# Softmax normalisation of an attention block split between VectorE and GpSimd, and spectra held back behind the last block of powers

## The chip, the cores and the metric

The kernel runs on one core of one Trainium2 chip. A core has engines that run side by side, each with an instruction queue of its own that it works through in order: TensorE (PE in the profile; PEld is its weight load), VectorE (DVE), ScalarE (ACT), GpSimd (POOL) and SyncE (SP), which here only issues DMAs. They wait for each other through semaphores. SBUF is the working memory. PSUM is the small memory that TensorE writes its results to. The metric is the device time of one execution in microseconds (us).

## The reference, cut to what matters

Two independent results stand side by side in the output. Both are over a sequence of 2048 positions and 448 channels, in float32.

```python
# A: a diagonal state-space model as a long convolution
dt = exp(log_dt); A = -exp(log_A_real) + 1j * A_imag
C = (C_real + 1j * C_imag) * dt[:, None]
P = exp((A * dt[:, None])[:, :, None] * pos)          # 448 x 256 x 2048 powers
K = 2.0 * einsum("dn,dnl->dl", C, P).real             # the kernel of the convolution
y = irfft(rfft(u, 2 * L) * rfft(K, 2 * L), 2 * L)[:L] + u * D_skip
# B: attention with 16 heads of 28
q, k, v = split(x @ wqkv)
p = softmax(q @ k.T * 28 ** -0.5)                     # per head, 2048 x 2048
out_B = (p @ v) @ wo
out = concatenate([y, out_B], axis=-1)
```

## The kernel before, in words

**Before the loop** the projections q, k and v and small tables ("seeds" of the powers, kept in DRAM as `sd`) are made. Nothing of that is touched.

**The loop** has 256 slots (variable `s`). Attention is cut into 16 units of 16 slots: unit `u` is a group of four heads (`u // 4`, four groups) and a quarter of the queries (`u % 4`, 512 queries). A slot takes 128 keys: four score matmuls (`pss`), four exponentials on ScalarE (`p`), and the sixteen matmuls with the values of the slot before (`po`). In the same slots the maxima of the scores of a later unit are found: four matmuls into `pm`, reduced on DVE (`mx`, `rl`). `pm` is a ring of three PSUM buffers in the loop, from `w_tile()`, which all other small matmuls share.

**Powers.** Between the attention work the kernel of the convolution is built in 56 blocks of 8 channels, one every 3.5 slots. For a block, ScalarE copies seeds into `e` and `g`. GpSimd then doubles `e` three times, with three instructions each time (`e_power`, line 689): `e<-e,sdb`, `eu<-e,sdb`, `e<-e,eu`, with 256, 512 and 1024 elements in each partition. So a block is nine GpSimd instructions. DVE does the like for `g`. Four slots after the block began, TensorE multiplies them (`pm<-e,g`, line 739), in two slots. The last block, 55, begins in slot 193.

**The end of a unit.** `fin` (line 789) copies the unit's sums `po` into `o`, whose layout has 32 rows for each head: 28 outputs and the denominator. Two functions are put in the list `free`, with the number of the call of `slot()` from which they are due; there are two such calls in a slot, three late in the loop. `sums` turns `o` in 32x32 squares on DVE (`rb<-o`), so that the denominators stand in columns, and takes the reciprocals `r`. `scale`, two calls later, turns the reciprocals back with DVE (`pm<-r`, into a ring buffer of PSUM), multiplies (`on<-o,pm`, DVE), and either stores `on` in DRAM (units 0 to 11) or puts the output projection in the list `p_due` (units 12 to 15, the last head group, `pm<-ua,og` and `pm<-ua,on`).

**Spectra and final transforms.** From slot 192 on, 16 jobs of kind `s` multiply the spectra of `u` and of the kernel (`spectrum`, line 828), and 8 jobs of kind `f` transform back (`finish`, line 871). A spectrum job makes `pm<-yk,mw` on TensorE twice, `pr<-pm,ub` on DVE, four products `p<-pr,pr` on GpSimd and `pm<-p,mw` on TensorE, whose result is stored. A final transform has a skip product `ut<-ut,dsk` on GpSimd and matmuls `pm<-zi,wb`. `f_slot` (line 980) takes the next task of such a job if the call of `slot()` had nothing more urgent.

**What sets the order.** In the loop every engine's instructions stay in the order in which the code issues them (`KEPT["a"]`, line 89). An engine may run ahead of the others, but never past an instruction of its own that waits. The lists `powers["e"]` and `powers["g"]` hold what is left of a block's powers; `k_due` holds the blocks that haven't begun.

Of the kernel before, what the change touches and what calls it, by code (L numbers as in the profile page):

```python
# [8 lines left out]
F32 = mybir.dt.float32  # L9
# [3 lines left out]
ALU = mybir.AluOpType  # L13
# [13 lines left out]
NK = L // 128  # L27
# [13 lines left out]
UG = (2, 2, 4)  # L41
# [51 lines left out]
def body(ctx, tc, a, out):  # L93
    nc = Engines(tc)
# [4 lines left out]
    def pool(stack, name, bufs=1, space=None, side=None):  # L99
        kw = {} if space is None else {"space": space}  # L100
        if side:
            kw["side"] = side
        return stack.enter_context(tc.tile_pool(name=name, bufs=bufs, reuse_waits="tile", **kw))
# [23 lines left out]
    def w_tile():  # L127

        n_ring[0] += 1
        return ps_w[0].tile([128, CQ], F32, name=f"pm{n_ring[0] % ps_w[1]}")  # L130
# [7 lines left out]
    def mm32(o, w, x_, start, stop, at=0):  # L138

        for i in range(w.shape[-1] // 32):  # L140
            c = slice(32 * i, 32 * i + 32)
            nc.tensor.matmul(o[c], w[:, c], x_, start=start, stop=stop, tile_position=(0, at + 32 * i))
# [467 lines left out]
    kq_p = pool(kq_st, "kq_p")  # L610
# [178 lines left out]
    def fin(u, s_):  # L789
        g, c = divmod(u, NQ)  # L790
        o = kq_p.tile([128, CQ], F32, name="o")
        nc.scalar.activation(o, o_u[u], AF.Copy)
        on = kq_p.tile([128, CQ], F32, name="on", bufs=2)
        og = og_u.pop(u, None)
        t_ = {}

        def sums():
            t = kq_p.tile([128, NK, 32], F32, name="rb")
            nc.vector.transpose(t.rearrange("p b e -> p (b e)"), o)
            t_["r"] = kq_p.tile([128, NK], F32, name="r", bufs=2)  # L800
            nc.vector.reciprocal(t_["r"], t[:, :, DH])

        def scale():
            pw = w_tile()
            nc.vector.transpose(pw.rearrange("p (b e) -> p b e", e=32), t_["r"][:, :, None].to_broadcast([128, NK, 32]))
            nc.vector.tensor_tensor(on, o, pw, ALU.mult)
            if g < G - 1:
                nc.sync.dma_start(on_d[c][g], on)
            else:
                p_due.extend((s_ + PD + PS * t, lambda t=t: project(t)) for t in range(4))  # L810

        def project(t):
            pw = w_tile()
            ts = slice(t * 128, (t + 1) * 128)
            for g2 in range(G):
                mm32(pw[:, :D], og[:, g2, ts] if g2 < G - 1 else on[:, ts], wo_t[g2 // 2][:, g2 % 2, :],
                     start=g2 == 0, stop=g2 == G - 1)
            y = kq_p.tile([128, D], F32, name="y", bufs=2)
            nc.scalar.activation(y, pw[:, :D], AF.Copy)
            q0 = c * CQ + t * 128  # L820
            nc.sync.dma_start(out[q0:q0 + 128, D:], y)

        free.append((n_slot[0] + UG[1], sums))
        free.append((n_slot[0] + UG[2], scale))

    fk = {}

# [83 lines left out]
    def job(j, p, uh_p, ps, b0=(2, 1, 1, 2, 2), b1=(2, 2)):  # L911
        kind, f, i = j
        return spectrum(f, i, p, uh_p, ps, b0) if kind == "s" else finish(f, i, p, ps, b1)
# [10 lines left out]
    urgent, free = collections.deque(), collections.deque()  # L924
    powers = {"g": collections.deque(), "e": collections.deque()}
# [20 lines left out]
    k_due = collections.deque(range(NB))  # L946
# [7 lines left out]
    n_slot, f_next = [0], {"s": 0, "f": 0}  # L954
# [6 lines left out]
    def f_load(s_, kind):  # L961

        if not f_jobs[kind] or f_loaded[kind]:
            return
        _, f, i = f_jobs[kind][0]
        if kind == "f" and s_done[0] < (f + 1) * N1 // 4:
            return
        if (kind, f, i) == ("f", 0, 0):
            if f_ready["s", 1] == NS:
                return  # L970
            f_p["f", 0] = f_p["f", 1] = pool(f1_st, "ff_p")
        if (kind, f) not in f_p or f_ready.get((kind, f), 0) > s_ + 2:
            return
        load, tasks, ahead = job(f_jobs[kind].popleft(), f_p[kind, f], kq_p, w_tile)
        load()
        if ahead:
            f_ahead.append((s_ + FL[kind] - 1, ahead))
        f_loaded[kind].append((max(f_ready.get((kind, f), 0), s_ + FL[kind]), tasks))

    def f_slot(s_, kind):  # L980
        f_load(s_, kind)
        while f_ahead and f_ahead[0][0] <= s_:
            f_ahead.popleft()[1]()
        if not f_tasks[kind]:
            if not f_loaded[kind] or f_loaded[kind][0][0] > s_:
                return False
            f_tasks[kind].extend(f_loaded[kind].popleft()[1])
            f_load(s_, kind)
        gap, t = f_tasks[kind][0]
        if n_slot[0] < f_next[kind] + gap:  # L990
            return False
        f_tasks[kind].popleft()
        t()
        s_done[0] += kind == "s" and not f_tasks[kind]
        f_next[kind] = n_slot[0]
        f_load(s_, kind)
        return True
# [10 lines left out]
    def slot(s_):  # L1008
        n_slot[0] += 1
        while free and free[0][0] <= n_slot[0]:  # L1010
            free.popleft()[1]()
        if urgent and urgent[0][0] <= n_slot[0]:
            urgent.popleft()[2]()
        elif s_ >= NS and f_slot(s_, "s"):
            pass
        elif p_due and p_due[0][0] <= s_:
            p_due.popleft()[1]()
        elif m_due and m_due[0][0] <= s_:
            m_due.popleft()[1]()
        elif u_due and u_due[0][0] <= s_:  # L1020
            u_part(*u_due.popleft()[1:])
        else:
            f_slot(s_, "s") or f_slot(s_, "f")
# [35 lines left out]
    for s in range(NS):  # L1059
# [26 lines left out]
        for op in ORDER:  # L1086
            if op[0] == "s":
                ps.append(s_mm(u, kt, int(op[1])))
            elif op[0] == "f":
                slot(s)  # L1090
            elif op[0] == "v":
                vec()
            elif op == "k":
                k_next()
                k_begin(s)
                k_seed(s)
                for _ in range(3):
                    if powers["e"]:
                        powers["e"].popleft()()
            elif op == "pv":  # L1100
                if prev:
                    pv_step(*prev)
                    if prev[1] == NK - 1:
                        fin(prev[0], s)
            elif sm < NS:
                max_mm(sm // NK, sm % NK, int(op[1]))
# [9 lines left out]
        prev = (u, kt, ps)  # L1116
    pv_step(*prev)
    fin(prev[0], NS)
    s = NS
    while urgent or free or p_due or m_due or u_due or any(q[k] for q in (f_jobs, f_tasks, f_loaded) for k in "sf"):  # L1120
# [61 lines left out]
```

## Time and profile before

| what | value |
|---|---|
| median of 3 runs | 1279.68 us (1278.78 to 1281.36) |
| the profiled execution | 1280.71 us |
| its span | 1278.9 us |
| granted TensorE clock, mean | 0.982 |
| DVE multiply `on<-o,pm` | 16 x 0.687 us |
| DVE transpose `pm<-r` | 16 x 0.720 us |
| POOL powers, a block | 9 instructions, 11.9 us (block 9: 349.54 to 361.43) |

A row of an engine in order of time reads: start in us from the span's start, length in us, engine, line, operation, output<-inputs, partitions x elements, how often; in brackets the idle time of the engine before it and whose work ended that wait. All work is issued through helpers, so every row has the line 77, and the names tell what it is. A row of the list by line has the busy time of all and the mean in ns, and behind the second bar the idle time before. A row of the list of waits reads: who waited for whom, us in total, times, longest.

### The profile page before, as it was taken

The page shows a single profiled execution, that of the slowest core. Times are in us where ns is not written, and L with a number is a line of the kernel's source. Part 1 is how long each engine was busy: PE and PEld are TensorE (multiplying, and loading weights), DVE is VectorE, ACT ScalarE, POOL GpSimd, SP SyncE. Part 2 cuts the span into 40 slices and gives each one's busy share as a digit, 9 for nine tenths or more (in the row PEclk, how much of TensorE's full clock was granted, in tenths as well). Part 3 has the DMA queues.
Part 4 walks back from the last instruction along what each step waited for, and adds up shares of the span by engine and source line. Part 5 has one row for each costly group of instructions (what it writes and reads, how often), then busy time and mean ns, then how long its engine had stood idle before and what let it go on. Part 6 is the DMA issues. An engine that isn't in the chain of part 4 may idle for free.

```text
span 1278.9 us, 31211 instructions
## 1 busy us (share of the span) xinstructions
PE 1199.8 (94%) x11569; PEld 669.9 (52%) x11569; DVE 942.6 (74%) x2138; ACT 959.2 (75%) x2146; POOL 843.5 (66%) x728
## 2 busy tenths in 40 slices
PE   6778887999999999999999999999997999999998
PEld 4667664555555555555555555555553545545333
DVE  5788966878777878887789889888996665646312
ACT  5888865788888888888888888888885766756553
POOL 2666740897788888778599999889984222424321
PEclk8999899899999999999999999999998999999999
DMA  6678789437554545365533133422314443647666
GB/s 195 215 254 297 268 287 358 120 88 195 155 147 115 164 118 178 110 228 178 170 88 104 49 88 103 148 82 71 99 43 141 157 161 135 210 151 236 201 179 164
DMA packets 203377, 206.08 MB, mean 161 GB/s; under 512 B 98201, under 2 KB 162265, under 8 KB 201177
## 3 DMA queue, kind: packets, MB, share of 16 engines
q1 hardware_dynamic: 202696, 203.50, 51.6%
q8 instruction: 91, 1.49, 0.5%
q10 hardware_dynamic: 528, 0.59, 0.2%
q14 instruction: 62, 0.50, 0.1%
HBM read 121.59 MB, written 82.18 MB: 159 GB/s over the span
## 4 chain that ended last, share of the span: by engine, by line
PE 72%; DVE 13%; POOL 5%; ACT 4%; issue 3%; DMA 2%; ACTq 0%; SPq 0%; POOLq 0%; DVEq 0%
PE pm L77 40%; PE pss L77 15%; PE po L77 15%; DVE mx L77 2%; DVE tri L77 2%; ACT rl L77 1%; ACT p L77 1%; DVE rl L77 1%; POOL qhat L77 1%; DVE g L77 1%; DVE zg L77 1%; POOL p L77 1%; DMA xn<-in_B_x 1%; POOL e L77 1%; PE pt L77 1%
## 5 line engine op out<-in xcount | busy, mean ns | idle before, releaser
L77 ACT ACTIVATE p<-pss 128x512 f32<-128x512 f32 x1024 | 561.9, 610 | 127.6 <-PE pss L77 124.3
L77 PE MATMUL pss<-qhat,khat 128*128 128x512 f32 x1024 | 402.0, 399 | 2.0 <-ACT p L77 2.0
L77 DVE TENSOR_REDUCE mx<-pm 128x1 f32<-128x512 f32 x480 | 308.2, 683 | 102.1 <-PE pm L77 100.5
L77 PE MATMUL pm<-khat,qhat 128*128 128x512 f32 x749 | 327.0, 440 | 14.3 <-DVE mx L77 5.4
L77 POOL TENSOR_TENSOR e<-e,sdb 128x256 f32<-128x256 f32 x168 | 201.9, 1202 | 110.8 <-ACT e L77 101.6
L77 PE MATMUL po<-p,v 128*32 128x512 f32 x2048 | 269.6, 595 | 0.0
L77 PEld LDWEIGHTS pm<-khat,qhat 128*128 128x128 f32 x749 | 140.9, 188 | 231.1 <-ACT p L77 53.7
L77 POOL TENSOR_TENSOR e<-e,eu 128x256 f32<-128x256 f32 x168 | 248.2, 1477 | 13.2
L77 DVE CUSTOM_DVE_ANT_0 rl<-pm,rl 128x512 f32<-128x512 f32 x259 | 178.1, 688 | 68.1 <-ACT rl L77 65.8
L77 PEld LDWEIGHTS pss<-qhat,khat 128*128 128x128 f32 x1024 | 190.4, 188 | 45.5 <-issue 11.4
L77 POOL TENSOR_TENSOR eu<-e,sdb 128x256 f32<-128x256 f32 x168 | 202.0, 1202 | 0.0
L77 POOL TENSOR_TENSOR p<-pr,pr 64x448 f32<-64x448 f32 x64 | 73.1, 1142 | 149.1 <-PE pm L77 108.1
L77 ACT ACTIVATE rl<-pm 128x512 f32<-128x512 f32 x259 | 156.7, 606 | 15.6 <-PE pm L77 9.4
L77 DVE TENSOR_TENSOR g<-g,zg 128x128 f32<-128x128 f32 x392 | 162.0, 413 | 3.5
L77 PE MATMUL pm<-kdif,qhat 128*128 128x512 f32 x249 | 100.0, 402 | 6.7 <-DVE xn L77 4.3
L77 PE MATMUL pm<-xh,khat 128*128 128x512 f32 x256 | 84.4, 422 | 11.9 <-DVE hl L77 5.1
L77 DVE TENSOR_TENSOR zg<-g,zg 128x128 f32<-128x128 f32 x224 | 87.9, 393 | 5.0
L77 PE MATMUL pm<-e,g 128*32 128x64 f32 x3584 | 73.7, 223 | 10.7 <-POOL e L77 8.2
L77 PEld LDWEIGHTS pm<-e,g 128*32 128x32 f32 x3584 | 56.0, 110 | 49.1 <-POOL e L77 12.5
L77 DVE TENSOR_TENSOR pr<-pm,ub 128x448 f32<-128x448 f32 x64 | 36.8, 618 | 45.8 <-PE pm L77 30.3
L77 ACT ACTIVATE y<-pm 128x448 f32<-128x448 f32 x48 | 26.6, 555 | 58.4 <-PE pm L77 32.8
L77 ACT ACTIVATE ub<-pm 128x224 f32<-128x224 f32 (+1 forms) x96 | 38.6, 448 | 40.0 <-PE pm L77 38.1
(132 smaller groups left out, 1406.1 us busy)
## 6 DMA issues: line engine op xcount, KB each, us to landing
sdb<-sd SPq DMA_DIRECT2D x55, 336.0 KB
qhat<-q SPq DMA_DIRECT2D x64, 256.0 KB
khat<-k SPq DMA_DIRECT2D x64, 256.0 KB
sd<-sg SPq DMA_DIRECT2D x8, 1456.0 KB
k<-hl SPq DMA_DIRECT2D x16, 512.0 KB
mw<-in_mw SPq DMA_DIRECT2D x16, 512.0 KB
sd<-qhat SPq DMA_DIRECT2D x8, 896.0 KB
yu_d<-ub SPq DMA_DIRECT2D x64, 112.0 KB
```

What stands on the lines that cost most here:

```text
L77: i = f(*args, **kw)
```

## The change

Three things are different.

1. `scale` is cut in two. `spread` comes at the call at which `scale` came, and turns the reciprocals back with DVE as before, but into SBUF (the buffer `rb`, which `sums` has used just before) and no longer into a PSUM buffer of the ring.
2. `scale` comes one call of `slot()` later and multiplies on GpSimd (`on<-o,rb`). The store of `on`, or the output projection, follows it there.
3. `f_slot` still loads what a spectrum or a final transform needs, but takes up no task as long as a block of powers is due or has instructions left.

```diff
+        def spread():
+            t_["rb"] = kq_p.tile([128, NK, 32], F32, name="rb")
+            nc.vector.transpose(t_["rb"], t_["r"][:, :, None].to_broadcast([128, NK, 32]))
+
         def scale():
-            pw = w_tile()
-            nc.vector.transpose(pw.rearrange("p (b e) -> p b e", e=32), t_["r"][:, :, None].to_broadcast([128, NK, 32]))
-            nc.vector.tensor_tensor(on, o, pw, ALU.mult)
+            nc.gpsimd.tensor_tensor(on, o, t_["rb"].rearrange("p b e -> p (b e)"), ALU.mult)
             if g < G - 1:
                 nc.sync.dma_start(on_d[c][g], on)
             else:
...
         free.append((n_slot[0] + UG[1], sums))
-        free.append((n_slot[0] + UG[2], scale))
+        free.append((n_slot[0] + UG[2], spread))
+        free.append((n_slot[0] + UG[2] + 1, scale))
...
     def f_slot(s_, kind):
         f_load(s_, kind)
+        if k_due or powers["e"] or powers["g"]:
+            return False
         while f_ahead and f_ahead[0][0] <= s_:
             f_ahead.popleft()[1]()
```

DVE's queue at the end of unit 1, before the change (numbers behind a name tell buffers apart):

```order
L77 TENSOR_TENSOR g_4318<-g_4318,zg_4390 128x32x8
L77 ISA rl_4497,mx_4134<-pm1_4503,rl_4497 128x512
L77 ISA mx_4134 128x1
L77 TENSOR_TENSOR g_4318<-g_4318,zg_4390 128x32x16
L77 STREAM_TRANSPOSE pm2_4511<-r_4436 128x512
L77 TENSOR_TENSOR on_4374<-o_4372,pm2_4511 128x512
L77 TENSOR_TENSOR zg_4390<-g_4318,zg_4390 128x256
```

In the changed program the transpose stands at the same place, with `rb` as its output, and the row with `on_4374` is gone from DVE. It is in GpSimd's queue, between the second and the third doubling of block 9:

```order
 L77 TENSOR_TENSOR eu_4472<-e_4255,sdb_3863 128x32x16
 L77 TENSOR_TENSOR e_4255<-e_4255,eu_4472 128x32x16
+L77 TENSOR_TENSOR on_4374<-o_4372,rb_4511 128x512
 L77 TENSOR_TENSOR e_4255<-e_4255,sdb_3863 128x32x32
 L77 TENSOR_TENSOR eu_4535<-e_4255,sdb_3863 128x1024
```

Three instructions of block 9 are now behind `on`, which reads what DVE's transpose writes. In the other units up to 11 it stands likewise ahead of the first, the fourth or the seventh instruction of a block.

GpSimd's queue at the last block of powers, 55 (`e_14134`), where unit 11 ends and the first spectrum's products (`p0`, `p1`) stood:

```order
 L77 TENSOR_TENSOR eu_14263<-e_14134,sdb_13785 128x32x8
 L77 TENSOR_TENSOR e_14134<-e_14134,eu_14263 128x32x8
+L77 TENSOR_TENSOR on_14193<-o_14191,rb_14304 128x512
 L77 TENSOR_TENSOR e_14134<-e_14134,sdb_13785 128x32x16
-L77 TENSOR_TENSOR eu_14351<-e_14134,sdb_13785 128x32x16
-L77 TENSOR_TENSOR e_14134<-e_14134,eu_14351 128x32x16
-L77 TENSOR_TENSOR p0_14414<-pr00_14345,pr11_14412 64x448
-L77 TENSOR_TENSOR p0_14414<-pr01_14347,pr10_14410 64x448
-L77 TENSOR_TENSOR p1_14417<-pr00_14345,pr11_14412 64x448
-L77 TENSOR_TENSOR p1_14417<-pr01_14347,pr10_14410 64x448
+L77 TENSOR_TENSOR eu_14332<-e_14134,sdb_13785 128x32x16
+L77 TENSOR_TENSOR e_14134<-e_14134,eu_14332 128x32x16
```

The four products now stand behind the whole block, and `on` of unit 11 ahead of its second doubling.

GpSimd's queue at the end of the program, in the change (`ut` are the skip products of the last final transforms):

```order
L77 TENSOR_TENSOR ut_17429<-ut_17429,dsk_16067 128x896
L77 TENSOR_TENSOR ut_17512<-ut_17512,dsk_16067 128x896
L77 TENSOR_TENSOR ut_17609<-ut_17609,dsk_16067 128x896
L77 TENSOR_TENSOR ut_17704<-ut_17704,dsk_16067 128x896
L77 TENSOR_TENSOR on_17746<-o_17744,rb_17760 128x512
L1184 UNCONDITIONAL_BRANCH
```

Before, the last `ut` was GpSimd's last work, and `on_17746` was DVE's.

## The prediction

> **What bounds the kernel now.** I read the page first, then who waited for whom, then the rows of single engines in order of time. The span and the busy shares:
>
> ```profile
> span 1278.9 us, 31211 instructions
> PE 1199.8 (94%) x11569; PEld 669.9 (52%) x11569; DVE 942.6 (74%) x2138; ACT 959.2 (75%) x2146; POOL 843.5 (66%) x728
> PE 72%; DVE 13%; POOL 5%; ACT 4%; issue 3%; DMA 2%; ACTq 0%; SPq 0%; POOLq 0%; DVEq 0%
> ```
>
> TensorE is busy for 94% and holds 72% of the chain that ended last. So an instruction that is moved between DVE and GpSimd is worth what it changes in TensorE's waits, not its own length. The waits that the change can touch:
>
> ```profile
> POOL e L77 <- ACT e L77: 101.6, 26, 39.8
> PE pm L77 <- POOL e L77: 8.2, 3, 6.5
> PE pm L77 <- DVE on L77: 4.4, 10, 0.7
> ```
>
> GpSimd's powers (`e`) wait for ScalarE's seeds 26 times: GpSimd runs ahead of its place in the program, by data. TensorE waits for powers only three times, 6.5 us of it once, and ten times, 4.4 us, for DVE's `on`, which holds one of three PSUM buffers.
>
> **Two DVE instructions become one, and one GpSimd instruction is added, 16 times.** The rows of the pair that the change takes apart, by line:
>
> ```profile
> L77 DVE STREAM_TRANSPOSE pm<-r 128x512 f32<-128x512 f32 x16 | 11.5, 720 | 0.0
> L77 DVE TENSOR_TENSOR on<-o,pm 128x512 f32<-128x512 f32 x16 | 11.0, 687 | 0.5
> L77 DVE STREAM_TRANSPOSE rb<-o 128x512 f32<-128x512 f32 x16 | 11.3, 705 | 1.1 <-ACT o L77 1.1
> ```
>
> The transpose stays, now into SBUF; the last row is a like transpose into SBUF, 0.705 us, so I keep 0.72. The multiply leaves DVE: 16 x 0.69 = 11.0 us, worth only what TensorE waited for it. On GpSimd its price is not in the trace. The nearest row is a 128x512 of the powers in the block of rows below, and is taken up there.
>
> **What stands behind the new instruction.** GpSimd works in order. That is seen where two clears wait behind TensorE:
>
> ```profile
> 626.77 0.85 POOL L77 MEMSET ua<- 128x896 f32 x1
> 638.78 0.85 POOL L77 MEMSET ua<- 128x896 f32 x1 [11.16 <-PE pm L77]
> ```
> ```profile
> 663.41 0.65 PE L77 MATMUL pm<-e,g 128*32 128x64 f32 x32 [1.33 <-POOL e L77]
> ```
>
> Two blocks of powers stand behind the second one; the later of them came 1.33 us too late for TensorE. The new `on` is such an instruction: it waits for DVE's transpose, and in units 0 to 11 powers are queued behind it, nine instructions to a block. One block's rows (block 9; instructions 1, 4, 6, 7 and 9):
>
> ```profile
> 349.54 0.63 POOL L77 TENSOR_TENSOR e<-e,sdb 128x256 f32<-128x256 f32 x1 [3.80 <-ACT e L77]
> 351.65 1.05 POOL L77 TENSOR_TENSOR e<-e,sdb 128x512 f32<-128x512 f32 x1
> 353.81 1.31 POOL L77 TENSOR_TENSOR e<-e,eu 128x512 f32<-128x512 f32 x1
> 355.19 1.91 POOL L77 TENSOR_TENSOR e<-e,sdb 128x1024 f32<-128x1024 f32 x1
> 359.05 2.38 POOL L77 TENSOR_TENSOR e<-e,eu 128x1024 f32<-128x1024 f32 x1
> ```
>
> The price of `on` first: a dense 128x512 takes 1.31 us (third row), one with a broadcast operand 1.05 (second). Both operands of `on` are dense, so I take 1.31. The block ends at 361.43. What is left of it is 11.89 us from its first instruction, 9.78 from the fourth, 6.24 from the seventh. The order of the changed program gives the place of `on`: ahead of the seventh of block 9 (unit 1), the fourth of 14 (unit 2), the fourth of 23 (unit 4), the first of 28 (unit 5), the seventh of 32 (unit 6), the first of 37 (unit 7), the seventh of 41 (unit 8), the fourth of 46 (unit 9), the fourth of 55 (unit 11).
>
> DVE's multiply in the trace starts 0.02 us after the transpose ended, so its start tells when GpSimd's may begin. These starts, units 1, 2, 4 to 9 and 11:
>
> ```profile
> 365.78 0.69 DVE L77 TENSOR_TENSOR on<-o,pm 128x512 f32<-128x512 f32 x1
> 430.39 0.69 DVE L77 TENSOR_TENSOR on<-o,pm 128x512 f32<-128x512 f32 x1
> 557.76 0.69 DVE L77 TENSOR_TENSOR on<-o,pm 128x512 f32<-128x512 f32 x1
> 622.06 0.69 DVE L77 TENSOR_TENSOR on<-o,pm 128x512 f32<-128x512 f32 x1
> 683.55 0.69 DVE L77 TENSOR_TENSOR on<-o,pm 128x512 f32<-128x512 f32 x1
> 739.98 0.69 DVE L77 TENSOR_TENSOR on<-o,pm 128x512 f32<-128x512 f32 x1
> 797.30 0.69 DVE L77 TENSOR_TENSOR on<-o,pm 128x512 f32<-128x512 f32 x1
> 854.78 0.69 DVE L77 TENSOR_TENSOR on<-o,pm 128x512 f32<-128x512 f32 x1
> 968.70 0.69 DVE L77 TENSOR_TENSOR on<-o,pm 128x512 f32<-128x512 f32 x1
> ```
>
> In unit 1 GpSimd went on to the seventh instruction at 355.19; now it must wait until 365.8. TensorE's first use of a block's powers, for blocks 9, 14, 23, 28, 32, 38, 42, 46 and 55:
>
> ```profile
> 371.90 0.65 PE L77 MATMUL pm<-e,g 128*32 128x64 f32 x32
> 440.11 0.65 PE L77 MATMUL pm<-e,g 128*32 128x64 f32 x32
> 567.82 0.65 PE L77 MATMUL pm<-e,g 128*32 128x64 f32 x32
> 636.42 0.65 PE L77 MATMUL pm<-e,g 128*32 128x64 f32 x32
> 689.39 0.65 PE L77 MATMUL pm<-e,g 128*32 128x64 f32 x32
> 762.98 0.65 PE L77 MATMUL pm<-e,g 128*32 128x64 f32 x32
> 813.26 0.65 PE L77 MATMUL pm<-e,g 128*32 128x64 f32 x32
> 864.11 0.65 PE L77 MATMUL pm<-e,g 128*32 128x64 f32 x32
> 987.42 1.08 PE L77 MATMUL pm<-e,g 128*32 128x64 f32 x32 [6.46 <-POOL e L77]
> ```
>
> The powers are ready at the start of `on` in the list, plus 1.5 us (1.31 and about 0.2 for three handovers), plus what is left of the block. Against TensorE's use:
> - unit 1: 365.78 + 1.5 + 6.24 = 373.52, late by 1.62
> - unit 2: 430.39 + 1.5 + 9.78 = 441.67, late by 1.56
> - unit 4: 557.76 + 1.5 + 9.78 = 569.04, late by 1.22
> - unit 5: 622.06 + 1.5 + 11.89 = 635.45, early by 0.97
> - unit 6: 683.55 + 1.5 + 6.24 = 691.29, late by 1.90
> - unit 7: block 38 follows block 37 without a gap, so 739.98 + 1.5 + 2 x 11.89 = 765.26, late by 2.28
> - unit 8: block 42 follows 41, so 797.30 + 1.5 + 6.24 + 11.89 = 816.93, late by 3.67
> - unit 9: 854.78 + 1.5 + 9.78 = 866.06, late by 1.95
>
> Units 0, 3 and 10 leave more room than unit 5. The seven late ones sum to **+14.2 us**, in which the loss of their waits for DVE is already counted. In units 0, 3, 5 and 10 those waits fall away for nothing in exchange: nine of 0.42 on average stand in the loop (4.4 less the last, 0.62, over nine), three of them in units 3, 5 and 10: **-1.3 us**. The next thing late there is DVE's transpose itself, which stays. On SP's queue the stores of `on` move back one slot; nothing behind them is needed within a slot.
>
> **The spectra that start later.** Before, the first spectrum's products came between the last block's powers:
>
> ```profile
> 968.75 0.96 PE L77 MATMUL pm<-yk,mw 128*32 128x224 f32 x16 [0.37 <-DVE pm L77]
> 976.35 4.77 POOL L77 TENSOR_TENSOR p<-pr,pr 64x448 f32<-64x448 f32 x4 [12.93 <-DVE pr L77]
> 987.00:992.00 5.00, 4.58 (x58) 2.26 (x59) 0.00 (x0) 0.53 (x2) 0.37 (x1) 0.56 0.00 0
> ```
>
> GpSimd held the last three powers of block 55 for 12.93 us until DVE's products came; TensorE stood 6.46 us and then ran at a granted clock of 0.56 (the row of the stretch from 987 to 992; the clock stands behind the busy times). With the spectra behind the powers this goes, but unit 11's `on` now stands ahead of the fourth instruction: 968.70 + 1.5 + 9.78 = 979.98. That is 7.4 us sooner than 987.42. Two groups of spectrum matmuls, about 0.9 us each, are moved behind it and are still to be done: 5.6 is left. The slow stretch costs 5 x (1 - 0.56) = 2.2 us; TensorE now waits at most 3 us there, nearest to the 1.33 us wait at 663.41, after which the same matmuls took 0.65 as always, so I count 2.2 as won. The two groups will meet the three PSUM buffers where they go: 1.0 us back (0.37 and two like it). Together **-6.8 us**, between -4 and -9.
>
> The Trainium skill ("TensorE: Matmul & The Clock Gate", Part 1) says that the clock falls to half after about 3.4 us without work. The rows fit: half after 6.46 us, full after 1.33, with nothing between them in the loop. By the page the new waits stay below it and the sum is the same; if unit 8's 3.67 us came in one piece it would add some 2 us by the page, but it falls on two blocks.
>
> In the changed order the last spectrum ends in slot 246 instead of 245, and from slot 249 TensorE's row of work is the same, so the moved work costs nothing unless its store is late for the first final transform.
>
> **The end.** For the last unit DVE's `on` let TensorE go at 1262.79; GpSimd has the skip product before it:
>
> ```profile
> 1260.36 2.09 POOL L77 TENSOR_TENSOR ut<-ut,dsk 128x896 f32<-128x896 f32 x1 [4.49 <-DVE ot L77]
> 1262.79 0.96 PE L77 MATMUL pm<-ua,on 128*32 128x448 f32 x8 [0.62 <-DVE on L77]
> ```
>
> 1262.45 + 1.31 + 0.14 = 1263.9: **+1.1 us**, all on the path. For units 12 to 14 `on` is needed only behind the matmuls of the three earlier head groups and has no powers behind it; it costs nothing, and without that cover 0.6 us a unit, the difference between the two multiplies.
>
> **The sum.** 14.2 - 1.3 - 6.8 + 1.1 = +7.2 us on the span of 1278.9. The profiled execution took 1280.71, 1.03 above the median of 1279.68; I put the difference on the median: 1286.9 us.
>
> **The rivals.**
> - *DVE turns the reciprocals sooner than the trace says* (place: the transpose ahead of `on`, units 1 to 9). Each microsecond sooner takes one from each of seven waits and adds one to the gain of unit 11, about 8 us in all, so from 0.9 us on the kernel is no longer slower; at 1.5 us it would take 1279.68 + 7.2 - 12 = 1274.9. For it: DVE has less to do. Against it: its transpose has 0.0 idle before it, and what it lost stands behind the transpose, not before it. 9%.
> - *GpSimd's `on` takes longer or is let go later than 0.1 us after the transpose.* By 0.5 us: 8 x 0.5 = +4, 1290.9. For it: DVE and GpSimd then work on SBUF at once. Against it: the powers keep 1.31 beside any DVE work. 14%.
> - *The change does not put the powers behind a wait, because GpSimd passes waiting instructions.* Then 1279.68 - 1.3 - 2.5 (the other six waits) - 6.8 + 1.1 = 1270.2. The clear at 638.78 speaks against it. 2%.
> - *The late spectra lengthen the end*: the first final transform of the second half waits for the last store; one slot, 3.3 us: 1290.2. 8%.
>
> **How the numbers follow.** The forecast has 67%, and itself runs from 1282 to 1291: 1.05 instead of 1.31 takes 7 x 0.26 = 1.8, the gain at block 55 moves by 2.8 either way. The range for 8 in 10 takes in most of the two slower rivals and the first half of the first: 1280 to 1292.5. About 0.2%, 2.6 us, is what a measurement of this kernel can tell from no change. Slower by more: most of the forecast and the two slower rivals, 83%; within it 8%; faster 9%, from the first and third rival.
>
> **What would show it.** GpSimd's `on` should stand with waits of 3 to 11 us for DVE ahead of it in units 0 to 11, and TensorE's waits for `e` should rise from 8.2 to some 18 us in about ten pieces, the largest below 4. Around the last block no wait of 6 us and no clock of 0.56. TensorE's waits for DVE's `on` should be gone, and the last one should be for GpSimd's. It is wrong if TensorE's use of a block is later than here by itself, or if DVE's transposes move.

## The result, and the profile after

The changed kernel takes 1296.08 us (median of 4 runs, 1294.2 to 1296.8), the kernel before 1280.49 us beside it (4 runs, 1278.78 to 1281.36). The ratio is 1.0122, with a 95% interval of 1.0109 to 1.0135: 15.6 us slower. Predicted were 1286.9 us, in a range that ended at 1292.5. The direction was right, and the size only half of what it is.

The head of the page of the kernel after (busy shares, then shares of the chain that ended last):

```profile
span 1294.2 us, 31215 instructions
...
PE 1203.9 (93%) x11569; PEld 672.9 (52%) x11569; DVE 932.7 (72%) x2122; ACT 959.5 (74%) x2146; POOL 861.8 (67%) x744
...
PE 64%; DVE 12%; POOL 10%; ACT 4%; issue 4%; DMA 4%; SPq 1%; ACTq 0%; POOLq 0%; DVEq 0%
```

GpSimd's busy time rose from 843.5 to 861.8 us, DVE's fell from 942.6 to 932.7, and GpSimd's share of the chain rose from 5% to 10%. What GpSimd does more is little; what counts is what TensorE waits for behind it. From the list of waits of the kernel after (who waited for whom, us in total, times, longest):

```profile
POOL on L77 <- DVE rb L77: 59.0, 9, 10.7
...
PE pm L77 <- POOL e L77: 21.9, 12, 2.8
...
PE pm L77 <- POOL on L77: 4.5, 2, 3.2
```

GpSimd waited 59.0 us in front of its multiply until DVE's transpose ended, and 23.1 us more in four waits that the list puts down to other engines. TensorE's waits for powers rose from 8.2 to 21.9 us in twelve pieces, its waits for DVE's `on` (4.4 us before) are gone, and two new ones, for GpSimd's `on`, are there. GpSimd's rows in order of time, kernel after, end of unit 1 (the last three rows are what is left of block 9):

```profile
352.55 1.30 POOL L77 TENSOR_TENSOR e<-e,eu 128x512 f32<-128x512 f32 x1
364.44 1.28 POOL L77 TENSOR_TENSOR on<-o,rb 128x512 f32<-128x512 f32 x1 [10.59 <-DVE rb L77]
365.67 1.91 POOL L77 TENSOR_TENSOR e<-e,sdb 128x1024 f32<-128x1024 f32 x1
...
369.54 2.34 POOL L77 TENSOR_TENSOR e<-e,eu 128x1024 f32<-128x1024 f32 x1
```

This is as predicted: 10.59 us of waiting, 1.28 us of work (1.31 was taken), and the block ends at 371.88 instead of 361.43. TensorE's rows behind it, kernel after:

```profile
371.93 0.65 PE L77 MATMUL pm<-e,g 128*32 128x64 f32 x32 [2.14 <-POOL e L77]
372.40 1.70 PE L77 MATMUL po<-p,v 128*32 128x512 f32 x8
373.85 1.74 PE L77 MATMUL pm<-ua,w 128*32 128x448 f32 x8
...
378.29 1.04 PE L77 MATMUL po<-p,v 128*32 128x512 f32 x8
```

TensorE waited 2.14 us. And then the same eight matmuls `po<-p,v` took 1.70 us that take 1.04 us one slot later. The clock says why: stretches of 4 us in both kernels (busy us of PE, PEld, DVE, ACT and POOL with counts, granted clock, DMA share, GB/s), first before, then after:

```profile
374.00:378.00 4.00, 4.00 (x54) 2.38 (x51) 3.03 (x7) 3.51 (x8) 0.31 (x2) 1.00 0.48 146
```
```profile
374.00:378.00 4.00, 4.00 (x32) 1.89 (x28) 1.61 (x3) 1.96 (x4) 3.84 (x4) 0.74 0.28 95
...
444.00:448.00 4.00, 4.00 (x16) 2.41 (x8) 2.08 (x5) 1.94 (x6) 3.76 (x5) 0.57 0.27 102
...
696.00:700.00 4.00, 4.00 (x46) 2.38 (x39) 1.43 (x3) 1.31 (x4) 3.77 (x6) 0.61 0.19 64
...
816.00:820.00 4.00, 4.00 (x57) 2.12 (x49) 2.77 (x6) 2.77 (x7) 3.77 (x5) 1.00 0.01 2
```

Behind the waits of 2.14, 2.17 and 2.46 us (blocks 9, 14 and 32) the granted clock fell to half for a while; behind one of 2.66 us, at 814.95, it stayed full. In the row from 444 the loss is 4 x (1 - 0.57) = 1.7 us. Each fall costs about that, and the three together 5.2 us, by the same working over all stretches of 4 us of the loop. The kernel before lost nothing there.

**Where the 15.3 us of the span are.** ScalarE's copy `o<-po` marks the end of each unit in both traces. The difference of its start to the kernel before tells how late a unit is, and the change of that difference what a stretch cost. The start at unit 0 itself moves by -0.97 to +0.62 us from run to run; that is scatter. For the end of unit 11, ScalarE's row of the kernel before, then of the kernel after:

```profile
961.09 0.71 ACT L77 ACTIVATE o<-po 128x512 f32<-128x512 f32 x1
```
```profile
975.68 0.73 ACT L77 ACTIVATE o<-po 128x512 f32<-128x512 f32 x1
```

At unit 0 the kernel after was 0.97 us early and here it is 14.59 late, so the loop cost 15.56. Every run of this study is cut up in this way (us against the trace of before; the last column is what the stretches and the start at unit 0 sum to):

| kernel | units 0 to 11 | 11 to 12 (block 55) | 12 to 13 | 13 to 14 | 14 to the end | span |
|---|---|---|---|---|---|---|
| after | +15.56 | -7.00 | +0.69 | +5.29 | +1.73 | +15.3 |
| e1: spectra alone | +0.02 | -10.55 | +0.95 | +0.96 | +0.89 | -8.2 |
| e2: GpSimd alone | +15.87 | +0.86 | +3.83 | -0.28 | +7.10 | +27.4 |
| e3: multiply 8 calls later | -7.12 | -11.28 | +0.67 | +1.69 | +1.96 | -14.0 |
| e4: last four units on DVE | +15.53 | -7.00 | +0.64 | +1.24 | +1.62 | +12.4 |
| e5: multiply 1 call later | -6.79 | -11.23 | +0.70 | +5.11 | +2.21 | -10.0 |
| e6: multiply 1 call earlier | +15.61 | -6.92 | +1.74 | +1.13 | +2.42 | +14.1 |
| e7: waits filled | +11.08 | -8.36 | +0.70 | +4.31 | +4.59 | +12.3 |
| e8: 8 calls later, last four on DVE | -7.14 | -11.28 | +0.92 | +1.02 | +2.11 | -15.0 |
| e9: DVE, both operands in SBUF | +4.01 | -9.65 | +1.00 | +2.29 | +1.73 | 0.0 |
| e10: e8 again | -7.00 | -11.26 | +0.91 | +1.17 | +1.89 | -14.1 |

### The profile page after: what moved, and what is told of

It reads as the page before. It is cut to its first block, busy times and chain, and to the rows that moved or that the text cites. A ratio compares the mean times of both kernels' runs of the same rounds, so it can differ in the third digit from the quotient of the medians.

```text
span 1294.2 us, 31215 instructions
## 1 busy us (share of the span) xinstructions
PE 1203.9 (93%) x11569; PEld 672.9 (52%) x11569; DVE 932.7 (72%) x2122; ACT 959.5 (74%) x2146; POOL 861.8 (67%) x744
## 4 chain that ended last, share of the span: by engine, by line
PE 64%; DVE 12%; POOL 10%; ACT 4%; issue 4%; DMA 4%; SPq 1%; ACTq 0%; POOLq 0%; DVEq 0%
PE pm L77 37%; PE po L77 13%; PE pss L77 13%; POOL e L77 4%; DVE mx L77 2%; DVE tri L77 2%; ACT rl L77 1%; POOL eu L77 1%; ACT p L77 1%; DVE rl L77 1%; POOL qhat L77 1%; DMA ut<-in_A_u 1%; DVE g L77 1%; DMA xn<-in_B_x 1%; DVE zg L77 1%
## 5 line engine op out<-in xcount | busy, mean ns | idle before, releaser
L77 PEld LDWEIGHTS pss<-qhat,khat 128*128 128x128 f32 x1024 | 192.1, 190 | 46.2 <-issue 10.6
L77 PE MATMUL pm<-e,g 128*32 128x64 f32 x3584 | 73.7, 223 | 21.9 <-POOL e L77 21.9
L77 POOL TENSOR_TENSOR on<-o,rb 128x512 f32<-128x512 f32 x16 | 20.6, 1285 | 82.2 <-DVE rb L77 59.0
```

The lines of the kernel that those rows point to most:

```text
L77: i = f(*args, **kw)
```

## The experiments

**The two halves alone.** First only the later spectra, with the softmax as before:

```diff
     def f_slot(s_, kind):
         f_load(s_, kind)
+        if k_due or powers["e"] or powers["g"]:
+            return False
```

> Only the third part of the change: the spectra wait until no block of powers is due or has instructions left; the multiply stays on DVE as before. Theory (waiting in GpSimd's queue): TensorE's wait of 6.46 us at block 55 and the slow clock behind it go, so about 9 us faster than before, less 1 to 2 us late in the loop where the later spectra meet: about 1273 us. Rival (the later spectra are what costs time at the end, from unit 12 on): the trace of the change lost 7 us from unit 12 to the end, and all of it would appear here: about 1279 us.

Measured: 1272.3 us, 0.9933 (0.9917 to 0.995). Then only the multiply on GpSimd, without these two lines:

> Only the first two parts: reciprocals into SBUF, multiply on GpSimd a slot later; spectra as before. Theory: the loss of units 0 to 10, 15.6 us, stays whole, and the stall at block 55 stays about as it was since the products hold the queue anyway; with unit 13 and the last unit, 3 to 6 us more: 1298 to 1302 us. Rival (the two parts of the change disturb each other and neither alone costs much): below 1290 us.

Measured: 1308.09 us, 1.0211 (1.0196 to 1.0226). So the loss belongs to the multiply, and the later spectra win: 8 to 9 us alone, 12 us beside the GpSimd multiply (1308.09 - 1296.08). The second run is 6 us slower than the expected range. In its trace `on` stands behind four spectrum products at units 12 and 14, TensorE waits 2.22 and 3.38 us for it, and the granted clock falls behind both; the stretches 12 to 13 and 14 to the end lost 3.8 and 7.1 us. TensorE at block 55 in e2:

```profile
1003.25 1.08 PE L77 MATMUL pm<-e,g 128*32 128x64 f32 x32 [6.47 <-POOL e L77]
```

The stall of the kernel before (6.46 us) is still there, and the matmuls behind it take 1.08 us, as before, in the place of 0.65. So it is the spectra's place that takes the stall away. In e1 the stretch of block 55 won 10.55 us; from unit 12 on it gave 2.8 back, with these waits of e1:

```profile
PE pm L77 <- POOL p L77: 3.3, 4, 1.4
...
PE pm L77 <- DMA zi<-z: 0.7, 1, 0.7
```

TensorE waits for GpSimd's spectrum products, four times, and once for a load of the first final transforms: the rival of the late spectra, in part.

**The queue's place.** In units 0 to 11 the multiply was put eight calls further back, behind the blocks of powers, everything else as in the change:

```diff
-        free.append((n_slot[0] + UG[2] + 1, scale))
+        free.append((n_slot[0] + UG[2] + (9 if g < G - 1 else 1), scale))
```

> The change with GpSimd's multiply of units 0 to 11 queued eight calls (four slots) later; the same instructions on the same engines, only the place in GpSimd's queue differs. Theory: DVE's transpose is then done when GpSimd comes to the multiply, no wait for DVE stands ahead of it, TensorE's waits for powers fall from 21.9 us to under 3 and the clock stays full in the loop; units 0 to 10 gain 15 to 19 us on the change and block 55 another 2 to 4: 1274 to 1279 us. Rival (GpSimd's longer multiply, or SBUF shared by DVE and GpSimd, is what slows the loop): the place doesn't matter, 1290 us or more.

Measured: 1267.53 us, 0.9899 (0.9885 to 0.9914), faster than expected. Next only one call, half a slot, further back (`+ 2` in the place of the 9):

> The change with GpSimd's multiply of units 0 to 11 one call (half a slot) later than in the change. In GpSimd's queue it then stands three instructions of the powers later: ahead of the fourth of block 5, the first of 10, the seventh of 14, 23, 46 and 55, the first of 33 and 42, the fourth of 37. Theory (powers queued behind the wait, priced as in the prediction: start in DVE's list + 1.5 us + what is left of the block): block 10 ready at 379.2 for 383.9, block 14 at 438.1 for 440.1, 23 at 565.5 for 567.8, 33 at 696.9 for 703.1, 42 at 810.7 for 813.3, 46 at 862.5 for 864.1, only block 38 late, by 0.2; so all of TensorE's waits of over 1.5 us go, and the clock with them: 1266 to 1270 us, like the multiply four slots later. Rival (the wait only shrinks by the half slot, about 1.9 us in each of seven places, and the clock still falls at the longest): 1275 to 1283 us.

Measured: 1270.0 us, 0.9919 (0.9904 to 0.9934). GpSimd's rows at the end of unit 1 in e5, and then the waits of e5:

```profile
365.37 1.28 POOL L77 TENSOR_TENSOR on<-o,rb 128x512 f32<-128x512 f32 x1 [4.45 <-PE pm L77]
366.61 0.64 POOL L77 TENSOR_TENSOR e<-e,sdb 128x256 f32<-128x256 f32 x1
```
```profile
POOL on L77 <- DVE rb L77: 31.4, 8, 6.0
...
PE pm L77 <- POOL e L77: 1.3, 1, 1.3
```

The first row names TensorE, but DVE's transpose had only just ended, at 365.22. Half a slot moved `on` from the middle of block 9 to the start of the next block. GpSimd still waits 31.4 us for the transpose at its multiply, but TensorE's waits for powers fell from 21.9 to 1.3 us. The same instruction on the same engine costs 26.1 us more or less (1296.08 - 1270.0), by what is queued behind it alone. The loop is 6.8 to 7.1 us faster than before in e3 and e5, where the sum had counted on 3.8 at most (TensorE's waits for DVE's `on` in the loop).

**The waits themselves or the clock.** TensorE got seven more matmuls ahead of the first use of `e` in seven late blocks. Their result is overwritten by the next matmul into the same buffer, so nothing is left out:

```diff
+FILL = (9, 14, 23, 32, 41, 46, 55)
...
+            if i == 0 and b in FILL:
+                u = now[0]
+                for _ in range(7):
+                    nc.tensor.matmul(pw, kt_g[u // NQ][0][:, :128], q_u[u][:, 0, :], start=True, stop=True)
...
+        now[0] = u
```

> The change with seven more score matmuls (about 1.6 us of TensorE work, written to the buffer that the block's own matmuls then overwrite) ahead of the first use of the powers of blocks 9, 14, 23, 32, 41, 46 and 55. More work for TensorE and no shorter wait for the powers. Theory (the waits of 2 to 3 us let TensorE's clock fall to half for 3.4 us, 1.7 us each, three times in the loop and once at block 55 in the change's trace): the work fits into the waits, the clock stays full, and the time falls by 5 to 7 us, to about 1290 us. Rival (the slow matmuls behind the waits are not the clock that follows idleness, or the added work meets no wait): the same as the change, or up to 11 us slower.

Measured: 1291.93 us, 1.0086 (1.0068 to 1.0103). With 49 matmuls more the kernel is 4.2 us faster than the change. TensorE at block 9 in e7, and then three stretches of e7, columns as above:

```profile
372.91 0.65 PE L78 MATMUL pm<-e,g 128*32 128x64 f32 x32 [0.56 <-POOL e L78]
373.38 1.04 PE L78 MATMUL po<-p,v 128*32 128x512 f32 x8
```
```profile
374.00:378.00 4.00, 4.00 (x56) 2.15 (x52) 2.07 (x4) 2.61 (x6) 3.77 (x5) 1.00 0.55 164
...
444.00:448.00 4.00, 4.00 (x54) 2.41 (x51) 3.27 (x9) 2.97 (x7) 3.84 (x4) 1.00 0.08 30
...
696.00:700.00 4.00, 4.00 (x52) 2.43 (x51) 3.90 (x11) 3.48 (x9) 3.84 (x4) 1.00 0.23 70
```

The powers come as late as in the change (TensorE's use at 372.91 instead of 371.93, with unit 0 ending 0.95 us later), but the clock is 1.00 in all three and `po<-p,v` takes 1.04 us. The loop cost 11.08 instead of 15.56 us, 4.5 less, near the 5.2 that the clock had taken. A part of that win was lost at the last unit, where TensorE waited 3.28 us for `on` behind the skip product and the clock fell.

**The last head group.** Two ways to take GpSimd's skip product from the path of `on` in units 12 to 15. In the first, DVE multiplies there, and GpSimd elsewhere:

```diff
-            nc.gpsimd.tensor_tensor(on, o, t_["rb"].rearrange("p b e -> p (b e)"), ALU.mult)
+            (nc.gpsimd if g < G - 1 else nc.vector).tensor_tensor(on, o, t_["rb"].rearrange("p b e -> p (b e)"), ALU.mult)
```

> The change with the multiply of units 12 to 15 back on DVE, still one call after the transpose into SBUF. Theory (at unit 13 the multiply waits on GpSimd behind a skip product that waits for a DMA): the wait of 3.19 us and the slow clock behind it go, and about 0.6 us at the very end: 5 to 6 us faster than the change, about 1290.5 us. Rival (the loss around unit 13 comes from the shifted spectra, not from the multiply): the same as the change within 1 us.

Measured: 1292.96 us, 1.0094 (1.0074 to 1.0115), 3.1 us less than the change and not 5 to 6; the intervals of the two overlap. The stretch from unit 13 to 14 did fall, by 4.05 us, but the profiled run was 1.3 us later at unit 0, which the edit does not touch, and the end gave 0.1 us and not 0.6. In the second GpSimd keeps all multiplies, one call earlier than in the change, in the call of the transpose:

```diff
-        free.append((n_slot[0] + UG[2] + 1, scale))
+        free.append((n_slot[0] + UG[2] + (1 if g < G - 1 else 0), scale))
```

> The change, with GpSimd's multiply of units 12 to 15 in the same call as the transpose; only the order of unit 13's multiply and the first skip product on GpSimd is turned round. Theory (at unit 13 the multiply waited behind a skip product that waited for a DMA): TensorE's 3.2 us and 1.7 us of slow clock go, the rest stays: about 1291 us. Rival (GpSimd's multiply is simply too slow for the cover of three head groups): the wait at unit 13 stays above 1 us and the time is within 2 us of the change.

Measured: 1295.7 us, 1.0122 (1.0107 to 1.0137), though the stretch from unit 13 to 14 fell from +5.29 to +1.13 as in e4 (+1.24). What happened in it: GpSimd and TensorE in the kernel after, where DVE's transpose had ended at 1127.71, and then TensorE in e6:

```profile
1127.00 0.71 DVE L77 STREAM_TRANSPOSE rb<-r 128x512 f32<-128x512 f32 x1
...
1129.94 2.07 POOL L77 TENSOR_TENSOR ut<-ut,dsk 128x896 f32<-128x896 f32 x1 [4.49 <-DMA dsk<-in_A_D_skip]
1131.97 1.26 POOL L77 TENSOR_TENSOR on<-o,rb 128x512 f32<-128x512 f32 x1
...
1133.28 1.25 PE L77 MATMUL pm<-ua,on 128*32 128x448 f32 x8 [3.19 <-POOL on L77]
```
```profile
1131.53 0.96 PE L77 MATMUL pm<-ua,on 128*32 128x448 f32 x8 [0.81 <-POOL on L77]
```

The first skip product waits for a load, `on` stands behind it, TensorE waits 3.19 us, and the matmuls behind it take 1.25 instead of 0.96 us. In e6 `on` stands ahead. (In e3, with the order of the change at this place, the stretch cost only 1.69 us: how long `on` is held there hangs on when the load lands.) That its total did not follow has no single cause in the trace: of the 4.2 us that it won there, it lost 1.1 ahead of unit 0, which the edit does not touch, and 1.1 at unit 12, where TensorE waited 0.80 us for `on`, and 0.7 behind unit 14.

**The ring buffer or DVE's time.** The loop's 7 us in e3 and e5 have two possible causes: a buffer of the ring is no longer held, or DVE has less to do. Here the spectra are held back and the transpose goes to SBUF, but DVE multiplies, in the same call, in all units:

```diff
-            nc.gpsimd.tensor_tensor(on, o, t_["rb"].rearrange("p b e -> p (b e)"), ALU.mult)
+            nc.vector.tensor_tensor(on, o, t_["rb"].rearrange("p b e -> p (b e)"), ALU.mult)
...
-        free.append((n_slot[0] + UG[2] + 1, scale))
+        free.append((n_slot[0] + UG[2], scale))
```

> The spectra held back; the reciprocals turned back into SBUF as in the change, but the multiply on DVE right behind, as before: no PSUM buffer of the ring is held, and DVE has all its work. The loop gained 7 us up to unit 11 where the multiply left DVE without a wait on GpSimd, against 0.5 us with the spectra held back alone; the prediction counted 3.8. Theory A (TensorE waited for the buffer of the ring): units 0 to 11 gain about 7 us here too: 1266 us. Theory B (it is DVE's 0.69 us, behind which the maxima of the ring's other buffers wait): no gain in the loop, about 1272 us.

Measured: 1280.77 us, 1.0001 (0.999 to 1.0012), the time of neither theory; the loop lost 4.0 us. The multiply itself had become slower. All 16 of it in e9 (ns least, median and most, first and last start), and then one of them with GpSimd's powers beside it, in e9 in order of time:

```profile
L77 DVE TENSOR_TENSOR on<-o,rb x16: 691/1203/2026, 301.0 to 1261.6; 128x512 f32<-128x512 f32 x16
```
```profile
299.82 1.92 POOL L77 TENSOR_TENSOR e<-e,sdb 128x1024 f32<-128x1024 f32 x1
...
301.03 1.25 DVE L77 TENSOR_TENSOR on<-o,rb 128x512 f32<-128x512 f32 x1
...
301.69 2.37 POOL L77 TENSOR_TENSOR eu<-e,sdb 128x1024 f32<-128x1024 f32 x1
```

With one operand in PSUM the multiply took 0.687 us every time. With both in SBUF it took 1.20 us in the median, and GpSimd's power beside it 2.37 instead of 1.92 us: the two held each other up. The Trainium skill ("SBUF — State Buffer", Terms and "SBUF: two separate sides") says that DVE and GpSimd share a pair of SBUF ports, that a DVE instruction with two SBUF inputs takes it for its whole length, and that the loser stands still. These rows agree in that both took longer; that one stood still they do not show. So the run does not hold DVE's time fixed. TensorE's waits in the loop, from unit 0 to unit 11, say more (before, then e9):

```profile
PE pm L77 <- DVE on L77: 3.8, 9, 0.7
PE pm L77 <- ACT rl L77: 1.9, 4, 0.6
```
```profile
PE pm L77 <- DVE mx L77: 15.3, 25, 2.0
```

The waits for `on` and for ScalarE's `rl`, 5.7 us together, are gone in e3 and in e9. In e9 waits for the maxima `mx` have come in their place, 15.3 us where before and e3 have 5.4 and 5.6; they stand some 10 us after the ends of units, behind the longer multiply. In two units of the loop that multiply took only 0.69 us: unit 3 won 0.40 us, as in e3 (0.44), and unit 10 lost 0.03 where e3 won 0.75. So how the 7 us split between the ring buffer and DVE's time is not settled. A rough estimate: the 11 multiplies of these stretches take 7.6 us of DVE before, 14.1 in e9 and none in e3. If the loop gets longer in proportion to that, +4.0 in e9 and -7.1 in e3 give 11.1 / 14.1 = 0.79 us for a us of DVE's work, and 1.1 us for the ring buffer. This estimate leaves out what e9 took from GpSimd, and the proportion does not hold unit by unit (in unit 0 the multiply took 1.25 us, and the stretch cost no more than in e3).

**The best of both.** The multiply on GpSimd behind the powers (e3) for units 0 to 11, and on DVE for the last four, at the call of the transpose:

```diff
-            nc.gpsimd.tensor_tensor(on, o, t_["rb"].rearrange("p b e -> p (b e)"), ALU.mult)
+            (nc.gpsimd if g < G - 1 else nc.vector).tensor_tensor(on, o, t_["rb"].rearrange("p b e -> p (b e)"), ALU.mult)
...
-        free.append((n_slot[0] + UG[2] + 1, scale))
+        free.append((n_slot[0] + UG[2] + (9 if g < G - 1 else 0), scale))
```

> The spectra held back; GpSimd's multiply of units 0 to 11 four slots later; the multiply of units 12 to 15 on DVE, in the same call as the transpose. Theory: as the multiply four slots later (1267.5 us), less 1.5 us at unit 13 and 1.1 us at the last unit: 1265 us. Rival: DVE's multiply in the end costs what GpSimd's did: 1267 us or more.

Measured: 1266.37 us, 0.9894 (0.9877 to 0.991). The same kernel again:

> The fastest kernel so far again, beside the one before it: 1266 us within 1 us.

Measured: 1265.68 us, 0.9883 (0.9862 to 0.9904). This version beats both kernels. Its waits (e8):

```profile
PE pm L77 <- POOL p L77: 3.6, 4, 1.4
...
PE pm L77 <- POOL e L77: 2.0, 2, 1.3
...
PE pm L77 <- DVE on L77: 1.0, 1, 1.0
```

Against e3 it is 1 to 2 us faster, within the intervals of both; the gain of the last edit is not settled.

## Why the prediction was wrong by half

Two terms that the sum put at nothing make up most of what it missed: the clock behind the new waits (5.2 us in the loop) and the multiply of unit 13 behind a skip product (4.2 us). A third, the relief of the loop, was too small by 3.3 us and hid a part of that. Step by step:

- **The mechanism and the waits in the loop: right.** TensorE's waits at the named blocks and their followers (9, 14, 23, 32, 37, 38, 41, 42, 46) are 2.14, 2.17, 1.70, 2.46, 0.88, 1.29, 2.66, 1.27 and 2.53, 17.1 us. The step said 14.2, with the waits for DVE that they replace (six of 0.42, 2.5) already taken off: 16.7 to be compared. That e5 takes all nine away by half a slot shows that the place in the queue is the cause.
- **"By the page the new waits stay below it and the sum is the same": the step that failed first.** The clock did not stay full. It fell behind three waits of 2.1 to 2.5 us, for 5.2 us in the loop, and e7 shows that this part goes away while the powers stay as late. The page that the step leaned on, "TensorE: Matmul & The Clock Gate", Part 1 of the Trainium skill, names some 3.4 us without work; here less was enough, and the measurement decides (how much less, the end of this section works out). The prediction's own rows had an empty stretch between 1.33 us (full) and 6.46 us (half), and six of its seven new waits fell into it. It should have kept a term for them: at 1.7 us a fall, seven waits could have cost up to 12.
- **Block 55, -6.8 us: right in sum (-7.0), wrong in a part.** The step counted 2.2 us of slow clock as won, nearest to a wait of 1.33 us. TensorE waited 2.80 us, and the clock was low once more (TensorE's row, then two stretches, kernel after):

```profile
994.42 1.08 PE L77 MATMUL pm<-e,g 128*32 128x64 f32 x32 [2.80 <-POOL e L77]
```
```profile
992.00:996.00 4.00, 1.58 (x36) 1.06 (x40) 0.48 (x2) 0.96 (x3) 2.33 (x1) 0.73 0.23 92
996.00:1000.00 4.00, 3.74 (x31) 1.65 (x23) 1.85 (x4) 1.13 (x3) 0.00 (x0) 0.84 0.00 0
```

That is 4 x 0.27 + 4 x 0.16 = 1.7 us lost. The start of this matmul was right: 994.42 less the 14.59 us by which the kernel after is late there is 979.83, and 979.98 was predicted. Without the multiply in front the stretch wins 10.6 us (e1) and 11.3 (e3, e5), so the later spectra are worth more than the 5.6 + 2.2 - 1.0 of the step. Two errors nearly cancel here; that the sum is right is in part luck.
- **"For units 12 to 14 ... it costs nothing": wrong for unit 13.** The step looked for powers behind `on` and for matmuls that cover it, not for what stands ahead of `on` in GpSimd's queue. There it was `ut`, waiting for a load: 3.19 us, and 1.7 us of slow clock. The stretch cost 5.3 us, and 1.0 in e1, 1.1 in e6 and 1.2 in e4, where `on` is not behind `ut`: about 4.2 us that the sum did not have. The step for the last unit had looked at just that queue, and its +1.1 came as a wait that grew from 0.62 to 1.30 us, 0.7 more (TensorE, kernel after):

```profile
1278.06 0.96 PE L77 MATMUL pm<-ua,on 128*32 128x448 f32 x8 [1.30 <-POOL on L77]
```

- **"-1.3 us" for the waits that fall away: too small.** The loop without late powers wins 7 us (e3, e5, e8) and not 3.8, all waits for `on` in the loop. The sum looked at these alone; four waits for ScalarE's `rl`, 1.9 us, fell away with them. Most of the rest is 1.4 us of TensorE's own busy time in the loop (655.1 us before, 653.7 in e3), for which no run shows a cause.
- **The rest of the sum.** The loop closes: -7.1 (e3) + 17.1 (waits) + 5.2 (clock) = 15.2, against 15.56 measured. From the forecast of +7.2 to the +15.3 of the span: +0.4 waits, +5.2 clock, -3.3 more relief, -0.2 at block 55 and +4.2 at unit 13 make 13.5. The other 1.8 are the start (-0.97) and small pieces behind block 55 of some 0.6 to 1.1 us a stretch, as e1 with its late spectra has them (0.9 to 1.0).
- **The rivals.** DVE's transposes did come a little sooner, 0.4 us at unit 1 (GpSimd's row at 364.44 and 0.97 for the earlier start, against 365.78), and nothing turned on it. GpSimd's `on` took no longer than the 1.31 us counted, by the list by tile of the kernel after (columns as for e9):

```profile
L77 POOL TENSOR_TENSOR on<-o,rb x16: 1261/1288/1303, 299.6 to 1276.7; 128x512 f32<-128x512 f32 x16
```

GpSimd passed no waiting instruction. The late spectra do lengthen the end, by 2.8 us in e1, inside a gain that is larger.

**Why the clock fell behind a wait of 2.14 us and not behind one of 2.66.** In every trace the granted clock changes only on a grid of 3.41 us. Taken along the steps of this grid, the kernel after reads (columns as above; two steps at block 9, then two at the wait that ends at 814.95):

```profile
369.24:372.65 3.41, 1.27 (x39) 0.71 (x41) 2.39 (x8) 1.80 (x4) 3.33 (x4) 1.00 0.85 198
372.65:376.06 3.41, 3.41 (x17) 0.94 (x10) 0.00 (x0) 0.64 (x2) 3.20 (x4) 0.50 0.59 187
```
```profile
812.97:816.38 3.41, 1.43 (x40) 0.60 (x40) 1.35 (x4) 0.95 (x3) 3.33 (x4) 1.00 0.46 171
816.38:819.80 3.42, 3.42 (x52) 2.03 (x48) 2.57 (x6) 2.56 (x7) 3.26 (x4) 1.00 0.01 2
```

The wait of 2.14 us lies in one step, whose idle time is 3.41 - 1.27 = 2.14 us, and the next step runs at 0.50. The wait of 2.66 us is split by a border, and 1.98 us of it lie in the step from 812.97; the next step stays at 1.00. In all twelve traces, from the end of unit 0 on, the clock fell after each of the 32 full-clock steps in which TensorE was idle for more than 2.03 us and after none of the 3391 with less than 1.76; of the six between, it fell after two. So a wait's place on the grid counts beside its length, and the place differs from run to run.

How the relief of the loop splits stays open.

## What to carry to other kernels

Before an instruction that waits is moved to an engine that runs ahead, list what is queued behind it there, and ahead of it too: here half a slot in GpSimd's queue was worth 26 us, and the multiply's own 1.3 us nothing. A TensorE wait of some 2 us may cost nearly twice its length, since the clock can fall behind it: such waits are priced with the clock, or bounded by it. One row of the same length at full clock does not settle it, since the place of the wait counts too. When an operand moves from PSUM to SBUF, price the instruction anew beside GpSimd's work.

## What the runs showed of the hardware that was not expected

- The granted TensorE clock fell to half behind waits of about 2 us and more, mostly for one step of 3.41 us and about 1.7 us of loss, but not behind all of them, and not behind the same ones in each run: in the change at blocks 9, 14, 32 and 55 and at unit 13, in e6, with nearly the same waits of the loop, in the stretches from 372, 692, 812 and 876. The shortest wait that it followed was 1.80 us (e9, at 1180.52), the longest that it did not follow 2.66. "TensorE: Matmul & The Clock Gate", Part 1 of the Trainium skill says that activity is watched in windows of 3413 ns that run freely. The traces agree: the clock changes on a grid of 3.41 us, and what counted was the idle time within one step.
- A DVE multiply of 128x512 in float32 took 0.69 us with one operand in PSUM, and 1.20 in the median, 2.03 at most, with both in SBUF beside GpSimd's work.
